# Dense products issued as one 128x128 matmul after a step of scores, in a two-round attention and feed-forward kernel

## The chip, the cores and the metric

The kernel runs on one core of one Trainium2 chip. The metric is the device time of one execution in microseconds. Before the change three runs gave 556.73, 559.66 and 559.98 us; the median, 559.66 us, is the time before.

## The reference, cut to what matters

There are 2048 tokens of width 512. One round is attention and then a gated feed-forward layer, each with a layer norm ahead of it and added to its input; two rounds run with the same weights.

```
x = x + _A_ref(_layernorm(x), A_wq, A_wk, A_wv, A_wo, A_beta)
x = x + _B_ref(_layernorm(x), B_w_gate, B_w_up, B_w_down)
x = x + _A_ref(...)      # the same again
x = x + _B_ref(...)
```

Attention has 32 heads of 16 channels. The tokens are cut into 4 segments of 512. Inside a segment it is causal softmax attention; beside it each head carries a memory over the segments: `M` (16x16) and `z` (16), from which `num = phi(q) @ M`, `den = phi(q) . z`, `a_mem = num / den`, and the result is `g * a_mem + (1 - g) * a_dot` with `g = sigmoid(beta)`. After each segment `M` and `z` grow by `phi(k)^T v` and the sum of `phi(k)`. The feed-forward layer is `gelu(x @ w_gate) * (x @ w_up) @ w_down` with 1792 hidden channels.

## The kernel before, in words

Two rounds of four segments make eight blocks `k = 0..7`. A block has projections to q, k and v, its steps of scores, the products of probabilities and values (called flushes in the code), from the second segment on the products with the memory, the output projection, and the feed-forward products gate, up and down.

All of it is put in order by a program that runs when the kernel is built. The class `Clocks` keeps an estimate of TensorE's clock, `ck.pe`, and of the other engines' clocks, and the loop at line 1620 chooses, at each value of `ck.pe`, the next piece of work for TensorE: a step of scores if its operands are there and four of the eight PSUM banks are free, else the next instruction of an open item, else a new item by its due time (`DUE`, `BIAS`), else a filler product of ones (`warm`) that keeps TensorE at work. A table `CHANGES` alters the due times and slacks at every 8 us of that clock. When the clock says that a result is there decides also which of VectorE and ScalarE empties a bank, and in which order these two, GpSimd and the DMA queue on SyncE get their work. The engines then run on the chip in the order that was built, each at its own pace, tied by semaphores.

TensorE's instructions use the 128x128 array in three shapes, which the text below calls by short names:

- **rows**: a step of scores (`visit`, line 1406, matmuls at line 1421). Four matmuls at once, each with 16 or 32 of the array's rows and all 128 columns (`tile_position=(32 * j, 0)`), one for each of four heads.
- **columns**: four matmuls at once, each with all 128 rows and 32 columns (`tile_position=(0, 32 * c)`). The flushes have this shape since each head has 32 output columns (line 1117, in `flush_item`), and in the kernel before so has every dense product: `product` (line 649, matmul at line 654) cuts one 128x128 product into four column strips. `dense` (line 656), `grown` (gate and up, line 1246), `piece` (down) and the filler call it, and so do the memory's products (`den_mm`, `mm` and `m` in `mem_items` and `upd_item`) and the transposes of `turn_item`.
- **whole**: one matmul with all rows and columns. In the kernel before only the 14 first fillers (line 552) and 16 transposes at the start (line 752) have it.

`Clocks.tiling(mode)` (line 338) adds `SWITCH = 0.108` us to `ck.pe` when the shape differs from the last one that was told to it; `visit` tells it "rows", `product` and `flush_item` tell it "columns".

Of the kernel before, what the change touches and what calls it, by code (L numbers as in the profile page):

```python
# [18 lines left out]
P = 128  # L19
# [7 lines left out]
KT = D // P  # L27
FF = 1792
FT = FF // P
# [430 lines left out]
def kernel(  # L460
# [14 lines left out]
    nc = tc.nc  # L475
# [52 lines left out]
    warm = cst.tile([P, P], BF16, name="warm")  # L528
    wide = warm[:].unsqueeze(1).to_broadcast([P, 4, P])
# [58 lines left out]
    def values_of(va, b, par, j):  # L588
        c = (16 * par + 4 * b + j) * (DH + 1)
        return slice(c, c + 32)  # L590
# [55 lines left out]
        ck.act.post(ck.made(), slack + tn.ACT_EVICT, (0.602, lambda: nc.scalar.activation(  # L646
            out=dst(), in_=src(), func=ACT.Copy), end), taken=taken)

    def product(out, lhsT, rhs, start=True, stop=True):

        ck.tiling("columns")
        for c in range(4):
            r = slice(32 * c, 32 * c + 32)
            nc.tensor.matmul(out[r], lhsT=lhsT[:, r], rhs=rhs, start=start, stop=stop, tile_position=(0, 32 * c))  # L654

    def dense(ps, pairs):
        n = len(pairs)
        return [(Clocks.MM[512], lambda i=i, l=l, r=r: product(ps()[:], l(), r(), i == 0, i == n - 1))
                for i, (l, r) in enumerate(pairs)]


# [106 lines left out]
    class Att:  # L768
# [319 lines left out]
        def flush_item(self, b, par, half):  # L1088
            k = self.k
            ps = Psum()  # L1090
            whole = half is None
# [18 lines left out]

            def mm():
                ck.tiling("columns")
                for n, (p, u, ki, q0, q1, step, c0) in enumerate(pieces):
                    shift = 0 if whole else HALF * p - HALF * half
                    va = vS if u == 2 else self.vaug
                    for j in range(4):
                        nc.tensor.matmul(ps()[32 * j:32 * j + 32, q0 + shift:q1 + shift],  # L1117
                                         lhsT=va[:, ki, values_of(va, b, p, j)],
                                         rhs=step["pt"][:, j, c0:c0 + q1 - q0], start=n == 0,
                                         stop=n == len(pieces) - 1, tile_position=(0, 32 * j))  # L1120
# [73 lines left out]
            rows = range(TPS) if whole or half else range(2)  # L1194
# [9 lines left out]
    class Ffn:  # L1204


        def __init__(self, k):
# [8 lines left out]
            def add_to_x(j, ps, slack, told, c=slice(0, D)):  # L1216
                xt, width = x_sb[:, self.tt0 + j, c], c.stop - c.start
                ck.dve.post(ck.made(), slack, (0.683 - 0.00104 * (D - width), lambda: nc.vector.tensor_tensor(  # L1218
                    out=xt, in0=xt, in1=ps()[:, 0:width], op=ALU.add), lambda t: (ps.read(t), told(t))))

            def loaded(name):
                return k > 0 or ("loaded", name) in ev
# [17 lines left out]
            def cols(h):  # L1240
                return slice(L * h // self.parts, L * (h + 1) // self.parts)

            def tiles(g):
                return range(self.parts * g, self.parts * g + self.parts)

            def grown(w, ps, g, h):
                return [(Clocks.MM[512] / self.parts + 0.0012 * (self.parts - 1),
                         lambda kt=kt, f=f, n=n: product(ps()[:, n * L // self.parts:(n + 1) * L // self.parts],
                                                         w[:, kt, f * P:(f + 1) * P], self.norm.xnT[:, kt, cols(h)],
                                                         kt == 0, kt == KT - 1))  # L1250
                        for n, f in enumerate(tiles(g)) for kt in range(KT)]

            def hidden(g, h):
# [62 lines left out]
            def down(j, c=slice(0, D)):  # L1316
                ps = Psum()
                h, width = j * self.parts // TPS, c.stop - c.start

                def piece(ft):  # L1320
                    product(ps()[:, 0:width], self.gel[:, ft, j * P:(j + 1) * P], wd_sb[:, ft, c], ft == 0, ft == FT - 1)
# [58 lines left out]
    def room_of(parts):  # L1380
        return both if sum(u == 2 for _, u, *_ in parts) > 1 else plain
# [24 lines left out]
    def visit(got):  # L1406
        k, t, parts, ends = streams.pop(0)
        a = att[k]
        step = room_of(parts).take()
        for i in got:  # L1410
            banks[i], owner[i] = 1e9, "s"
        for b, u, ki, q0, q1, c0 in parts:
            a.pts[b, u, ki, q0] = (q1, step, c0)
            step["left"] |= a.uses[b, u, ki, q0]
            for j in range(4):
                rows = slice(32 * j, 32 * j + (32 if u else 16))
                if u == 2:
# [3 lines left out]
                nc.tensor.matmul(big[:, got[j], c0:c0 + q1 - q0], lhsT=lhsT, rhs=a.q[rows, b, q0:q1], start=True,  # L1421
                                 stop=True, tile_position=(32 * j, 0))
        ck.tiling("rows")
        begun = ck.pe
        ck.on_pe(ck.STEP + ck.PART * (len(parts) - 2))
        width = max(c0 + q1 - q0 for _, _, _, q0, q1, c0 in parts)
        even = WHOLE and got[3] - got[0] == 3
        exp_and_mask(step, parts, got, [slice(0, 4)] if even else [slice(0, 2), slice(2, 4)], width, begun + 0.4)
        for f in ends:
            a.flush_item(*f)  # L1430
        if not any(st[0] == k for st in streams):
            ev["scores", k] = ck.pe
        if not any(st[0] == k and any(part[1] == 2 for part in st[2]) for st in streams):
            ev.setdefault(("shared", k), ck.pe)
# [185 lines left out]
    while streams or items or opened or ck.busy():  # L1620
        if tn.turn(ck.pe):
            items.sort(key=tn.due)
        ck.serve()
        next_e()
        if step_ready() and four_banks() and timely():
            score()
            continue
        if opened:
            cost, fn = opened.ops.pop(0)
            fn()  # L1630
            ck.on_pe(cost)
            if not opened.ops:
                it, opened = opened, None
                it.done()
            continue
        if may_open():
            late = ck.pe - tn.FLUSH_WAIT
            got = next((it for it in items if (it.kind != "flush" or not streams or it.posted < late
                                               or plain.full() or both.full()) and it.ready()), None)
            if got:  # L1640
                opened = open_item(got)
                continue
        if may_open():

            if streams:
                ps = Psum()
                ps.bank = free_banks()[-1]
                owner[ps.bank] = "m"
                product(ps()[:], warm[:], wide)
# [35 lines left out]
```

## Time and profile before

| what | number |
| --- | --- |
| runs, lowest / median / highest | 556.73 / 559.66 / 559.98 us |
| profiled execution: span from first to last instruction | 554.7 us |
| median less that span | 5.0 us |
| TensorE busy (PE) | 540.0 us, 97% of the span, 13722 matmuls |
| VectorE (DVE) / ScalarE (ACT) / GpSimd (POOL) busy | 432.6 / 419.6 / 237.9 us |
| 16 DMA engines, mean rate | 55 GB/s |
| granted TensorE clock | 1.000 |

How to read it: the page gives the profiled execution its span, and the three runs are whole device times, so a time is the span and some 2 to 5 us around it. PE is TensorE's matmuls and PEld its weight loads. In a row of the trace, "L654" is a line of the kernel, "128\*32" the array's rows and columns that a matmul uses, "128x512" its output, "x16" how many such matmuls were merged; the first two numbers are the start and the length in us. The end of a matmul is modelled, and it lies behind the start of the next one, so a length from a row overstates the time that the matmul keeps the array; the distance between two starts does not.

### The profile page before, as it was taken

The numbers are of one execution on the slowest core, as the hardware profiler recorded it, in microseconds if no ns is written. First come the engines' busy times: TensorE is split into PE (matmuls) and PEld (weight loads), VectorE is DVE, ScalarE is ACT, GpSimd is POOL, SyncE is SP. The second block draws the span as 40 slices with busy tenths as digits, with TensorE's granted clock in tenths as the row PEclk, the third lists the DMA queues.
The fourth block names the chain that finished last, engine by engine and source line by source line (L and its number), as shares of the span: only waits on it lengthen the run. The fifth ranks groups of instructions, "written<-read, shape, count | busy, mean of one in ns | idle before, by whom it ended". The sixth has DMA issues, their size and how long they took to land.

```text
span 554.7 us, 29909 instructions
## 1 busy us (share of the span) xinstructions
PE 540.0 (97%) x13722; PEld 293.8 (53%) x13722; DVE 432.6 (78%) x830; ACT 419.6 (76%) x386; POOL 237.9 (43%) x416
## 2 busy tenths in 40 slices
PE   8999899989899999999999999999999999999997
PEld 4446754765345444454444444445455455545994
DVE  7998689869897978688896876589988697588162
ACT  3899789988799887977989787968869855960610
POOL 6469045257348334834475345164582334112000
PEclk9999999999999999999999999999999999999999
DMA  8767527013601132300315020333242004010001
GB/s 258 182 144 183 101 56 95 14 22 59 83 4 21 23 60 42 59 8 19 55 28 70 14 41 4 50 51 24 40 98 61 2 5 98 6 20 21 24 5 41
DMA packets 69775, 30.39 MB, mean 55 GB/s; under 512 B 55120, under 2 KB 69200, under 8 KB 69648
## 3 DMA queue, kind: packets, MB, share of 16 engines
q1 hardware_dynamic: 69504, 28.46, 26.8%
q8 instruction: 107, 1.75, 1.3%
q14 instruction: 20, 0.16, 0.1%
q10 hardware_dynamic: 144, 0.01, 0.0%
HBM read 9.71 MB, written 2.10 MB: 21 GB/s over the span
## 4 chain that ended last, share of the span: by engine, by line
PE 80%; DVE 9%; DMA 4%; ACT 3%; issue 2%; POOL 1%; SPq 0%; ACTq 0%; DVEq 0%; POOLq 0%
PE big L654 68%; PE big L1421 7%; PE big L1117 5%; ACT pt L1491 3%; DMA amT<-am 1%; DVE xn L713 1%; DVE byq L1145 1%; DVE st L677 1%; DMA xnT<-xn 1%; DVE ab L1153 1%; POOL pt L1464 1%; DMA vS<-vaug 1%; DMA x_sb<-in_A_x_dram 1%; DVE x_sb L1218 1%; DVE aT L1160 1%
## 5 line engine op out<-in xcount | busy, mean ns | idle before, releaser
L1491 ACT ACTIVATE pt<-big 128x2048 bf16<-128x2048 f32 (+1 forms) x151 | 272.8, 1810 | 68.8 <-PE big L1421 63.7
L1464 POOL TENSOR_SCALAR_AFFINE_SELECT pt<-pt 64x256 bf16<-64x256 bf16 (+4 forms) x302 | 151.9, 530 | 232.7 <-ACT pt L1491 231.4
L654 PE MATMUL big<-xnT,wu_sb 128*32 128x512 bf16 (+1 forms) x2240 | 105.6, 337 | 0.9 <-issue 0.9
L654 PE MATMUL big<-wd_sb,gel 128*32 128x512 bf16 (+2 forms) x1848 | 105.2, 373 | 0.0
L654 PE MATMUL big<-xnT,wg_sb 128*32 128x512 bf16 (+1 forms) x2240 | 104.7, 337 | 0.0
L1308 DVE TENSOR_TENSOR gel<-gel,big 128x512 bf16<-128x512 bf16 x112 | 75.0, 682 | 32.0 <-PE big L654 26.9
L654 PEld LDWEIGHTS <-wg_sb 128*32 128x32 bf16 x2240 | 57.5, 97 | 35.6 <-issue 4.6
L654 PEld LDWEIGHTS <-wu_sb 128*32 128x32 bf16 x2240 | 58.2, 97 | 34.1 <-issue 4.9
L654 PEld LDWEIGHTS <-gel 128*32 128x32 bf16 x1848 | 46.6, 97 | 43.3 <-issue 3.6
L1218 DVE TENSOR_TENSOR x_sb<-x_sb,big 128x512 bf16<-128x512 bf16 (+1 forms) x65 | 43.1, 668 | 25.6 <-PE big L654 25.3
L1145 DVE STREAM_TRANSPOSE byq<-big 128x512 f32<-128x512 f32 x64 | 45.2, 706 | 20.5 <-PE big L1117 20.0
L1117 PE MATMUL big<-pt,vaug 128*32 128x64 bf16 (+5 forms) x1152 | 45.0, 263 | 2.1 <-issue 1.9
L677 DVE BATCH_NORM_STATS2 st<-x_sb 128x6 f32<-128x512 bf16 x60 | 40.5, 675 | 0.4
L1273 ACT ACTIVATE gel<-big 128x512 bf16<-128x512 f32 x64 | 35.2, 605 | 4.5 <-PE big L654 4.3
L654 PE MATMUL big<-xnT,wq_sb 128*32 128x512 bf16 (+1 forms) x528 | 35.0, 373 | 2.0 <-DMA xnT<-xn 1.7
L654 PE MATMUL big<-xnT,wk_sb 128*32 128x512 bf16 (+2 forms) x528 | 34.4, 373 | 0.0
L654 PE MATMUL big<-wo_sb,aT 128*32 128x512 bf16 x512 | 32.3, 380 | 0.1
L654 PE MATMUL big<-wv_sb,xnT 128*32 128x512 bf16 x512 | 31.9, 380 | 0.0
L816 POOL TENSOR_SCALAR kS<-kf,maskA 128x256 bf16<-128x256 bf16 x28 | 29.3, 1046 | 3.7 <-PE big L1421 2.6
L816 POOL TENSOR_SCALAR kS<-kf,maskB 128x256 bf16<-128x256 bf16 x28 | 29.1, 1041 | 0.3
L1117 PE MATMUL big<-pt,vS 128*32 128x64 bf16 x960 | 28.0, 193 | 1.2 <-DMA vS<-vaug 1.2
L713 DVE TENSOR_SCALAR xn<-x_sb,mv,rs 128x512 bf16<-128x512 bf16 x64 | 27.3, 471 | 1.1 <-POOL rs L1509 0.9
(98 smaller groups left out, 643.0 us busy)
## 6 DMA issues: line engine op xcount, KB each, us to landing
vS<-vaug SPq DMA_DIRECT2D x16, 136.0 KB, 2.7
out_dram<-x_sb SPq DMA_DIRECT2D x15, 128.0 KB, 2.7
wg_sb<-in_B_w_gate_dram SPq DMA_DIRECT2D x8, 224.0 KB, 5.6
wu_sb<-in_B_w_up_dram SPq DMA_DIRECT2D x8, 224.0 KB, 3.8
kB<-kf SPq DMA_DIRECT2D x28, 64.0 KB, 2.6
wd_sb<-in_B_w_down_dram SPq DMA_DIRECT2D x7, 256.0 KB, 4.7
x_sb<-in_A_x_dram SPq DMA_DIRECT2D x3, 512.0 KB, 6.4
xnT<-xn SPq DMA_TRANSPOSE x48, 3.1
```

What stands on the lines that cost most here:

```text
L654: nc.tensor.matmul(out[r], lhsT=lhsT[:, r], rhs=rhs, start=start, stop=stop, tile_position=(0, 32 * c))
L677: nc.vector.bn_stats(out=self.st6[:, 0, :], in_=x_sb[:, self.tt0 + j, :])
L713: eng.tensor_scalar(out=xn[:], in0=x_sb[:, self.tt0 + j, :], scalar1=self.mv[:, j, 0:1], scalar2=self.rs[:, j, :], op0=ALU.subtract, op1=A ...
L816: eng.tensor_scalar(out=kS[:, b, :, :, u], in0=self.kf[:, b, :].rearrange("p (t h c) -> p t h c", h=2, c=Q)[:, :, 0, :], scalar1=(maskA, m ...
L1117: nc.tensor.matmul(ps()[32 * j:32 * j + 32, q0 + shift:q1 + shift], lhsT=va[:, ki, values_of(va, b, p, j)], rhs=step["pt"][:, j, c0:c0 + q ...
L1145: nc.vector.transpose(out=self.byq[:, c], in_=ps()[:])
L1218: ck.dve.post(ck.made(), slack, (0.683 - 0.00104 * (D - width), lambda: nc.vector.tensor_tensor(out=xt, in0=xt, in1=ps()[:, 0:width], op=A ...
L1273: return lambda: nc.scalar.activation(out=out(), in_=in_(), func=ACT.Gelu_apprx_tanh)
L1308: ck.dve.post(ck.made(), NORMAL, (0.683, lambda: nc.vector.tensor_tensor(out=hidden(g, h), in0=hidden(g, h), in1=banked(ps), op=ALU.mult), ...
L1421: nc.tensor.matmul(big[:, got[j], c0:c0 + q1 - q0], lhsT=lhsT, rhs=a.q[rows, b, q0:q1], start=True, stop=True, tile_position=(32 * j, 0))
L1464: nc.gpsimd.affine_select(out=v, in_=v, pattern=[[0, m], [by, size]], compare_op=ALU.is_ge, fill=0.0, base=by - 1, channel_multiplier=-1)
L1491: 0.172 + 0.000832 * width * len(banks_of), lambda g=g, st=st: nc.scalar.activation(out=pt[:, g, 0:width], in_=st, func=ACT.Exp, scale=SCA ...
```

## The change

Dense products get a new argument, `dense=True`, and a variable `array` remembers which shape TensorE was last given. A dense product is issued as one whole matmul if the shape is not "columns", that is from a step of scores on, until a flush or one of the memory's products (or a transpose) sets it back to "columns". After that, dense products are cut into four strips as before, until the next step of scores. On the whole branch `product` returns ahead of `ck.tiling("columns")`, so there the planner's clock is not told of any shape.

```diff
-    def product(out, lhsT, rhs, start=True, stop=True):
+    def product(out, lhsT, rhs, start=True, stop=True, dense=False):
 
+        if dense and array[0] != "columns":
+            array[0] = "whole"
+            nc.tensor.matmul(out, lhsT=lhsT, rhs=rhs, start=start, stop=stop)
+            return
+        array[0] = "columns"
         ck.tiling("columns")
         for c in range(4):
             r = slice(32 * c, 32 * c + 32)
             nc.tensor.matmul(out[r], lhsT=lhsT[:, r], rhs=rhs, start=start, stop=stop, tile_position=(0, 32 * c))
 
+    array = ["columns"]
...
     def dense(ps, pairs):
...
-lambda i=i, l=l, r=r: product(ps()[:], l(), r(), i == 0, i == n - 1))
+lambda i=i, l=l, r=r: product(ps()[:], l(), r(), i == 0, i == n - 1, True))
...
# flush_item, mm():
                 ck.tiling("columns")
+                array[0] = "columns"
...
# visit(), behind the matmuls of the scores:
         ck.tiling("rows")
+        array[0] = "rows"
...
# grown (gate, up), piece (down) and the filler of the main loop: the same True (dense=True)
```

In the changed kernel the whole branch's matmul is line 653, the strips' line 659, the scores' line 1429 and the flushes' line 1125. TensorE has 10009 matmuls (13722 before): 1243 of them are whole dense products, 1094 with an output of 128x512 and 149 with one of 128x256. The following rows are TensorE's instructions in program order; `aT`, `wq_sb`, `wk_sb` are operands of dense products, `kB`, `kf` of scores, `pt` and `vaug` of flushes.

First, TensorE behind a step of scores in block 0, before: the last matmul of the scores and one dense product (of the output projection), in four strips.

```order
L1421 MATMUL big<-q,kB_130 128x192
L654 LDWEIGHTS aT
L654 MATMUL big<-wo_sb,aT 32x512
L654 LDWEIGHTS aT
L654 MATMUL big<-wo_sb,aT 32x512
L654 LDWEIGHTS aT
L654 MATMUL big<-wo_sb,aT 32x512
L654 LDWEIGHTS aT
L654 MATMUL big<-wo_sb,aT 32x512
```

TensorE behind the same step of scores in the changed kernel:

```order
L1429 MATMUL big<-q,kB_130 128x192
L653 LDWEIGHTS wq_sb
L653 MATMUL big<-xnT,wq_sb 128x512
L653 LDWEIGHTS wq_sb
L653 MATMUL big<-xnT,wq_sb 128x512
L653 LDWEIGHTS wq_sb
L653 MATMUL big<-xnT,wq_sb 128x512
L653 LDWEIGHTS wk_sb
```

Each dense product is now one load and one matmul, and it is another product that stands there: a projection of the next block in place of the output projection.

Second, TensorE where dense products end and a flush begins, before (block 0, the key projection and then the flush):

```order
L654 LDWEIGHTS wk_sb
L654 MATMUL big<-xnT,wk_sb 32x512
L1117 LDWEIGHTS vaug_132
L1117 MATMUL big<-pt,vaug_132 32x256
L1117 LDWEIGHTS vaug_132
```

Such a place in the changed kernel (the query projection, then the flush):

```order
L653 LDWEIGHTS wq_sb
L653 MATMUL big<-xnT,wq_sb 128x512
L1125 LDWEIGHTS vaug_132
L1125 MATMUL big<-pt,vaug_132 32x256
L1125 LDWEIGHTS vaug_132
```

Before, both sides were columns and nothing changed shape between them; now the shape changes from whole to columns ahead of the flush.

Third, TensorE early in block 0, where the order itself moved. Before, the step of scores over `kB` is followed by projections:

```order
L1421 LDWEIGHTS kB_130
L1421 MATMUL big<-q,kB_130 128x256
L654 LDWEIGHTS wq_sb
L654 MATMUL big<-xnT,wq_sb 32x512
L654 LDWEIGHTS wq_sb
```

In the changed kernel the next step of scores follows it at once:

```order
L1429 LDWEIGHTS kB_130
L1429 MATMUL big<-q,kB_130 128x256
L1429 LDWEIGHTS kf
L1429 MATMUL big<-q,kf 128x256
L1429 LDWEIGHTS kf
```

The projections of queries and keys moved behind the next scores and their flush. From there on the two orders differ all along the program, on every engine, though each has the same dense products, scores and flushes; the changed one has 4 filler products more (53 in place of 49).

Counted over the whole of each order, the shape changes from one TensorE matmul to the next as follows:

| from > to | before | changed |
| --- | --- | --- |
| columns > rows | 145 | 85 |
| rows > columns | 144 | 26 |
| rows > whole | 1 | 117 |
| whole > rows | 0 | 58 |
| whole > columns | 3 | 61 |
| columns > whole | 1 | 1 |
| all | 294 | 348 |

More of the change, by code (lines that the diff above doesn't have):

```diff
@@ L654, in product @@
             nc.tensor.matmul(out[r], lhsT=lhsT[:, r], rhs=rhs, start=start, stop=stop, tile_position=(0, 32 * c))
+    array = ["columns"]
     def dense(ps, pairs):
         n = len(pairs)
-        return [(Clocks.MM[512], lambda i=i, l=l, r=r: product(ps()[:], l(), r(), i == 0, i == n - 1))
+        return [(Clocks.MM[512], lambda i=i, l=l, r=r: product(ps()[:], l(), r(), i == 0, i == n - 1, True))
                 for i, (l, r) in enumerate(pairs)]
@@ L1249, in grown @@
                                                          w[:, kt, f * P:(f + 1) * P], self.norm.xnT[:, kt, cols(h)],
-                                                         kt == 0, kt == KT - 1))
+                                                         kt == 0, kt == KT - 1, True))
                         for n, f in enumerate(tiles(g)) for kt in range(KT)]
@@ L1320, in piece @@
                 def piece(ft):
-                    product(ps()[:, 0:width], self.gel[:, ft, j * P:(j + 1) * P], wd_sb[:, ft, c], ft == 0, ft == FT - 1)
+                    product(ps()[:, 0:width], self.gel[:, ft, j * P:(j + 1) * P], wd_sb[:, ft, c], ft == 0, ft == FT - 1, True)
                 def told(t):
@@ L1648 @@
                 owner[ps.bank] = "m"
-                product(ps()[:], warm[:], wide)
+                product(ps()[:], warm[:], wide, dense=True)
                 ck.unread(Clocks.MM[512])
```

## The prediction, made before the changed kernel ran

> **What bounds the kernel now.** I read the page's busy shares first, then its chain of work that ended last.
>
> ```profile
> PE 540.0 (97%) x13722; PEld 293.8 (53%) x13722; DVE 432.6 (78%) x830; ACT 419.6 (76%) x386; POOL 237.9 (43%) x416
> ...
> PE 80%; DVE 9%; DMA 4%; ACT 3%; issue 2%; POOL 1%; SPq 0%; ACTq 0%; DVEq 0%; POOLq 0%
> PE big L654 68%; PE big L1421 7%; PE big L1117 5%; ACT pt L1491 3%; DMA amT<-am 1%; DVE xn L713 1%; DVE byq L1145 1%; DVE st L677 1%; DMA xnT<-xn 1%; DVE ab L1153 1%; POOL pt L1464 1%; DMA vS<-vaug 1%; DMA x_sb<-in_A_x_dram 1%; DVE x_sb L1218 1%; DVE aT L1160 1%
> ```
>
> TensorE has work for 97% of the span, and 80% of the chain is TensorE, 68% the dense products that the change touches. A share is a mean over stages, so I asked next for the busy time by stretch (columns: stretch, its length, then PE, PEld, DVE, ACT, POOL).
>
> ```profile
> 40.00:110.00 70.00, 65.22 (x2036) 43.05 (x2036) 58.83 (x123) 62.04 (x62) 31.04 (x53) 1.00 0.49 91
> 110.00:180.00 70.00, 66.17 (x1836) 35.90 (x1832) 56.84 (x107) 61.75 (x61) 40.57 (x60) 1.00 0.26 37
> 180.00:250.00 70.00, 69.67 (x1648) 34.30 (x1644) 57.76 (x107) 58.29 (x46) 33.01 (x59) 1.00 0.21 39
> 460.00:530.00 70.00, 70.00 (x1824) 43.12 (x1816) 41.94 (x81) 39.16 (x43) 10.19 (x29) 1.00 0.15 32
> ```
>
> From 180 us on TensorE is nearly without a gap. Between 40 and 180 us it waits for 4.78 + 3.83 = 8.6 us, and there ScalarE, with 62 of 70 us, is next in line. The clock is 1.00 throughout. TensorE's waits are small and few:
>
> ```profile
> PE big L654 <- issue: 2.9, 4, 1.5
> PE big L1117 <- issue: 1.9, 1, 1.9
> PE big L654 <- DMA xnT<-xn: 1.7, 3, 0.8
> PE big L1117 <- DMA vS<-vaug: 1.2, 1, 1.2
> ```
>
> So the time is the sum of what TensorE does, and what the change does to that sum is what it does to the time, unless it makes new waits.
>
> **What a change of shape costs.** "Busy" hides one thing: a matmul's record reaches past the start of the next one. The timeline of starts shows it.
>
> ```profile
> 16.14 1.05 PE L654 MATMUL big<-xnT,wq_sb 128*32 128x512 bf16 x16
> 17.01 1.05 PE L654 MATMUL big<-xnT,wk_sb 128*32 128x512 bf16 x16
> ...
> 27.05 1.90 PE L654 MATMUL big<-warm 128*32 128x512 bf16 x32
> 28.88 0.29 PE L1421 MATMUL big<-q,kf 16*128 16x256 bf16 x4
> 29.00 0.28 PE L1421 MATMUL big<-q,kB 32*128 32x256 bf16 x4
> 29.21 1.05 PE L654 MATMUL big<-xnT,wq_sb 128*32 128x512 bf16 x16
> ```
>
> Four products (16 strips) take 17.01 - 16.14 = 0.87 us from start to start: 0.216 us for a product in columns, 0.108 for half the width. The 8 fillers from 27.05 on are through at 27.05 + 8 x 0.216 = 28.78, and the scores start at 28.88: columns > rows costs 0.10 us. The last scores, 256 wide, need 0.108 from 29.00 on, to 29.11, and the projection starts at 29.21: rows > columns costs 0.10 as well. The same in the middle of the program:
>
> ```profile
> 202.34 1.68 PE L654 MATMUL big<-wo_sb,aT 128*32 128x512 bf16 x28
> 203.95 0.40 PE L1421 MATMUL big<-q,kB 32*128 32x64 bf16 x8
> 204.28 1.26 PE L654 MATMUL big<-wo_sb,aT 128*32 128x512 bf16 x20
> ```
>
> Seven products end at 202.34 + 1.51 = 203.85, scores at 203.95 (0.10); the step is 64 + 448 = 512 columns wide in all, 0.216, and 0.33 us pass until the next product (0.11). I take 0.10 us for each change, from 0.09 to 0.11. With 294 changes (the table of front) the kernel before spends 29 us, 5% of its span, on changing shape.
>
> **The change part by part.**
>
> *The products themselves.* The trace has whole products only at the start. The last fillers of line 552, at the full clock, in the timeline:
>
> ```profile
> 5.29 1.03 PE L552 MATMUL big<-warm 128*128 128x512 bf16 x4
> ```
>
> Four fillers take 1.03 us, of which the last record is some 0.38 (in the row at 16.14, 1.05 less three starts of 0.216 leaves 0.40): three starts in 0.65, 0.216 us each. A whole product keeps the array as long as four strips, weight load included, so the 1243 products that become whole gain and lose nothing. For the 149 of half the width I take 0 too, since the 128-wide whole transposes of line 752 start every 0.06 us (next fence). TensorE gets 3713 matmuls fewer; that could shorten the waits marked "issue", 4.8 us at most, and I keep it among the waits.
>
> *Changes of shape that the trace shows.* Whole > columns goes from 3 to 61, columns > rows from 145 to 85, rows > columns from 144 to 26. The last two cost 0.10 us as above. For the first, and for the pair that matters most, there is this stretch of the timeline:
>
> ```profile
> 9.62 0.41 DVE L713 TENSOR_SCALAR xn<-x_sb,mv,rs 128x512 bf16<-128x512 bf16 x1
> ...
> 9.76 0.29 PE L1421 MATMUL big<-q,kB 32*128 32x256 bf16 x4
> ...
> 10.08 0.40 PE L752 MATMUL big<-ident,xn 128*128 128x128 bf16 x4
> ...
> 10.70 0.40 PE L752 MATMUL big<-ident,xn 128*128 128x128 bf16 x4 [0.21 <-DVE xn L713]
> ...
> 11.02 0.62 PE L654 MATMUL big<-warm 128*32 128x512 bf16 x8
> ```
>
> Their lengths, in the answer on line 752 (shortest, median, longest in ns):
>
> ```profile
> L752 PE MATMUL big<-ident,xn x16: 219/219/230, 6.5 to 10.9; 128*128 128x128 bf16 x16
> ```
>
> The four transposes at 10.70 last 0.40 us with a last record of 0.219, so they start every 0.06 us and are through at 10.94; the filler in columns starts at 11.02. Whole > columns costs 0.08 to 0.09 us; I take 0.10 for it too.
>
> *Changes that it does not show.* Rows > whole goes from 1 to 117 and whole > rows from 0 to 58: 175 changes on which the answer hangs. The one of before stands in the fence: the scores at 9.76 need 0.108 us, to 9.87, and the transposes start at 10.08, 0.21 later. But their operand `xn` comes from VectorE at 9.62 + 0.41 = 10.03, so the 0.21 may be all wait. The price lies between 0 (nothing in the row excludes it) and 0.21. Between these ends I take 0.10, because every change that can be seen, three pairs with three different partners, costs 0.08 to 0.11, with little regard to what the shapes on either side are.
>
> The page "TensorEngine Tiling (Array Packing)" of the Trainium skill says under Key Properties that a change of tiling mode, not of the tile alone, drains TensorE, and its list of configurations has 128x128, 32x128 and 128x32 as three modes. The trace agrees for the three pairs above; no run here shows it for rows and whole. By that rule the change adds a drain ahead of most flushes and removes none, which is the forecast below.
>
> *The sum of the shapes.* 348 changes in place of 294, each 0.10 us: **+5.4 us**. The mechanism is plain: a stretch scores, products, scores has two changes of shape in either kernel; a stretch scores, products, flush, scores had two and now has three, since the products are no longer in the shape that the flush needs.
>
> *Fillers.* Four more, 4 x 0.216: **+0.9 us**.
>
> *The order.* On the whole branch the planner's clock is told no shape, so it no longer charges its 0.108 us there, and the order differs from block 0 on (the third pair of rows in front shows projections that moved behind the next scores and their flush). The same work is in both lists; what can differ is how long TensorE waits. If TensorE really pays for the changes that the planner leaves out, it runs later than planned, and the other engines have that much more time to feed it; so I expect no crowd of new waits. The bounds: down, the "issue" waits shrink, -3; up, the 6% of waits between 40 and 180 us reach 100 us further, +6. I take **+1 us**, near the middle, since the rows after 180 us show hardly any. ScalarE, the next engine in line, has the same steps to turn into exponentials, and the queues of SyncE and GpSimd carry the same transfers and masks, in another order.
>
> Together +7.3 us on the span of 554.7, so 562.0, and 5.0 around it as at the median: **567.0 us**, 1.3% slower. Its own range, with 0.08 to 0.12 for the 175 unseen changes (3.5 us either way) and the waits' ends, is 561 to 575.
>
> **The rivals.**
>
> *Rows and whole need no drain between them* (the other side). Both use all 128 columns undivided, and only the rows taken differ; the row at 10.08 allows it. Then 175 of the 348 changes are free and 173 remain: 17.3 us in place of 29.4, -12.1; fillers +0.9. Here the planner is right about TensorE, which runs faster, so waits grow between 40 and 180 us, where ScalarE already has 89% of the time: +5. Sum -6.2: **553.5 us**, from 548.5 to 559. Against it: no seen change is free, though one side of the pair whole > columns also has all its rows in use. The point from which it decides: with p for an unseen change, 173 x 0.10 + 175 p - 29.4 + 0.9 is zero at p = 0.064 us without new waits, at 0.04 with 4 us of them. Below that the kernel is faster.
>
> *Only one of the two directions is free.* Free into whole: 231 changes, -6.3 + 0.9 + 3 of waits, 557.3. Free out of whole: 290, -0.4 + 0.9 + 2, 562.2. For it: a drain may depend on what runs out. Against it: columns > rows and rows > columns cost alike.
>
> *The order is what costs.* As the forecast, but the projections arrive late all along and TensorE waits after 180 us too as it does between 40 and 180, at 6% over 130 us more: +7.8, **574.8 us**. For it: the two orders agree for the first steps only. Against it: TensorE's long run without a gap from 180 us on, in which VectorE and ScalarE have 58 of 70 us (the row from 180 to 250).
>
> *The change doesn't do what it says:* it says that the order is untouched, and the lists of instructions say otherwise; that is in the sums above. That the products do become whole is seen in the rows.
>
> **How the numbers follow.** A measurement of this kernel tells about 1% from no change: faster is under 554.1, slower over 565.3. Forecast 0.54, of which 0.39 lies over 565.3 and 0.15 under. Rows and whole free 0.30: 0.17 faster, 0.13 within 1%. One direction free 0.10, all within 1%. The order 0.06, slower. That gives faster 0.17, same 0.38, slower 0.45. The range goes from 551 (most of the free case) to 575 (the end of the forecast's range, which cuts the order's case in half).
>
> **What would show it.** In the profile after: behind a step of scores that waits for nothing, the first whole product starts 0.10 us after the scores' columns are streamed; by the rival it starts at once, with its weight load ahead of it beside the scores. Ahead of a flush that follows whole products there is a new 0.10 us. Whole products start every 0.216 us; if they start further apart, the first step of the sum is wrong. TensorE's waits between 40 and 180 us should stay near 8.6 us; twice that, or waits behind 180 us, and the order decides. A span under 550 us would mean that the 175 changes are free or nearly so.

## The result, and the profile after

Four runs of the changed kernel gave 563.51, 564.62, 566.40 and 566.50 us, a median of 565.51; four of the kernel before (the three above and 558.46) gave a median of 559.06. The ratio to before is 1.0136, with a 95% interval from 1.0095 to 1.0178. The change makes the kernel slower by 6.5 us; the forecast was +7.3 us on the span and 567.0 us. The sum came out nearly right, but two of its terms did not, and they had opposite signs; that is what the rest is about.

The page of the changed kernel: busy shares, the granted clock in 40 slices of 14 us, the queue that brings instructions (packets, MB, share), and the chain.

```profile
span 564.8 us, 22454 instructions
PE 550.5 (97%) x10009; PEld 281.1 (50%) x10009; DVE 431.9 (76%) x827; ACT 420.8 (75%) x388; POOL 235.4 (42%) x420
PEclk9999998799899999999999999999999999999999
q8 instruction: 78, 1.28, 1.0%
PE 91%; DVE 3%; ACT 3%; DMA 1%; POOL 1%; issue 1%; ACTq 0%; DVEq 0%; POOLq 0%
PE big L653 46%; PE big L659 30%; PE big L1429 8%; PE big L1125 7%; ACT pt L1500 2%; DMA xnT<-xn 1%; DVE x_sb L1226 1%; DMA x_sb<-in_A_x_dram 1%; DVE st L684 0%; DVE xn L720 0%; DVE byq L1153 0%; DVE st L1514 0%; POOL rs L1518 0%; DVE xnT L645 0%; ACT L1281 0%
```

TensorE is still the bound: 91% of the chain, where it had 80%. It has a quarter fewer matmuls and is busy 10.5 us longer. New are the 8, 7 and 8 in the row of the clock. The same stretches as before (length, then PE, PEld, DVE, ACT, POOL, granted clock, DMA share, GB/s):

```profile
40.00:110.00 70.00, 66.49 (x1194) 38.22 (x1196) 55.35 (x114) 59.55 (x60) 29.16 (x50) 0.93 0.47 90
110.00:180.00 70.00, 67.24 (x1453) 35.20 (x1449) 57.71 (x108) 61.16 (x57) 40.44 (x61) 0.98 0.19 35
180.00:250.00 70.00, 70.00 (x1182) 32.05 (x1175) 54.86 (x103) 60.75 (x55) 32.52 (x56) 1.00 0.22 38
460.00:530.00 70.00, 69.60 (x1323) 37.17 (x1325) 47.80 (x98) 36.85 (x34) 12.45 (x30) 1.00 0.15 32
```

Between 40 and 180 us TensorE waits 3.51 + 2.76 = 6.3 us (8.6 before), and behind 180 us hardly at all, as predicted. Its waits are other ones, though (us in total, times, longest):

```profile
PE big L1125 <- ACT pt L1500: 3.7, 2, 1.8
PE big L659 <- DMA xnT<-xn: 2.7, 1, 2.7
PE big L552 <- DVE warm L530: 1.1, 1, 1.1
...
PE big L659 <- issue: 0.3, 1, 0.3
```

The waits marked "issue", 4.8 us before, are down to 0.3; in their place stand two waits of 1.8 us for exponentials and one of 2.7 us for a transposed block. What comes with the latter shows in short stretches of the same kernel:

```profile
90.00:95.00 5.00, 2.31 (x112) 1.41 (x103) 4.28 (x9) 3.07 (x3) 2.32 (x6) 0.94 0.72 111
95.00:100.00 5.00, 4.18 (x61) 1.47 (x61) 1.70 (x3) 2.37 (x2) 0.78 (x2) 0.50 0.02 4
100.00:105.00 5.00, 5.00 (x75) 2.30 (x72) 3.39 (x8) 2.91 (x4) 0.78 (x2) 0.54 0.28 56
105.00:110.00 5.00, 5.00 (x90) 3.94 (x91) 4.37 (x7) 4.97 (x5) 0.78 (x2) 1.00 0.14 26
```

From 94.4 to 104.6 us TensorE is granted half its clock, and "busy" there is half the work. The 10.2 us of it cost up to 5.

**The price of the changes of shape after**, in the timeline of TensorE's starts:

```profile
69.08 1.03 PE L653 MATMUL big<-xnT,wq_sb 128*128 128x512 bf16 x4
70.04 0.29 PE L1125 MATMUL big<-pt,vaug 128*32 128x256 bf16 x4
...
199.74 1.67 PE L653 MATMUL big<-wd_sb,gel 128*128 128x512 bf16 x7
201.35 0.40 PE L1429 MATMUL big<-q,kf 16*128 16x320 bf16 x8
...
203.86 0.41 PE L1429 MATMUL big<-q,kS 32*128 32x64 bf16 x32
204.20 2.12 PE L653 MATMUL big<-wv_sb,xnT 128*128 128x512 bf16 x9
```

Whole > columns: four products end at 69.08 + 0.864 = 69.94, the flush starts 0.10 later. Whole > rows: seven products and the change take 201.35 - 199.74 = 1.61 us; before, seven in columns and the change took the same 1.61 (202.34 to 203.95). Rows > whole: a step over `kS` and the change take 0.34; before, the same step with columns behind it took

```profile
116.06 0.41 PE L1421 MATMUL big<-q,kS 32*128 32x64 bf16 x32
116.40 0.51 PE L654 MATMUL big<-xnT,wu_sb 128*32 128x256 bf16 x12
```

0.34 too. Over all starts of this kernel that waited for nothing, at the full clock and with 0.216 us taken for 512 columns, rows > whole costs 0.09 us (111 of them), whole > rows and columns > rows 0.096, whole > columns 0.093 and rows > columns 0.09. The pair that no row of before showed costs what all others cost.

### The profile page after: what moved, and what is told of

It reads as the page before. It is cut to its first block, busy times and chain, and to the rows that moved or that the text cites. A ratio compares the mean times of both kernels' runs of the same rounds, so it can differ in the third digit from the quotient of the medians.

```text
span 564.8 us, 22454 instructions
## 1 busy us (share of the span) xinstructions
PE 550.5 (97%) x10009; PEld 281.1 (50%) x10009; DVE 431.9 (76%) x827; ACT 420.8 (75%) x388; POOL 235.4 (42%) x420
## 4 chain that ended last, share of the span: by engine, by line
PE 91%; DVE 3%; ACT 3%; DMA 1%; POOL 1%; issue 1%; ACTq 0%; DVEq 0%; POOLq 0%
PE big L653 46%; PE big L659 30%; PE big L1429 8%; PE big L1125 7%; ACT pt L1500 2%; DMA xnT<-xn 1%; DVE x_sb L1226 1%; DMA x_sb<-in_A_x_dram 1%; DVE st L684 0%; DVE xn L720 0%; DVE byq L1153 0%; DVE st L1514 0%; POOL rs L1518 0%; DVE xnT L645 0%; ACT L1281 0%
## 5 line engine op out<-in xcount | busy, mean ns | idle before, releaser
L653 PE MATMUL big<-xnT,wg_sb 128*128 128x512 bf16 (+1 forms) x374 | 75.8, 354 | 0.1
L653 PE MATMUL big<-wd_sb,gel 128*128 128x512 bf16 x233 | 55.0, 380 | 0.0
L653 PE MATMUL big<-xnT,wu_sb 128*128 128x512 bf16 (+1 forms) x259 | 54.8, 356 | 0.0
L653 PEld LDWEIGHTS <-wg_sb 128*128 128x128 bf16 x374 | 34.7, 98 | 34.3 <-issue 4.3
L659 PE MATMUL big<-xnT,wu_sb 128*32 128x256 bf16 (+1 forms) x1204 | 51.5, 321 | 0.0
L659 PE MATMUL big<-wd_sb,gel 128*32 128x512 bf16 (+2 forms) x916 | 49.9, 366 | 0.0
L659 PEld LDWEIGHTS <-wu_sb 128*32 128x32 bf16 x1204 | 32.2, 97 | 11.3
L653 PEld LDWEIGHTS <-wu_sb 128*128 128x128 bf16 x259 | 23.2, 98 | 23.5 <-issue 4.2
L659 PEld LDWEIGHTS <-gel 128*32 128x32 bf16 x916 | 24.7, 97 | 18.0
L659 PE MATMUL big<-xnT,wg_sb 128*32 128x256 bf16 (+1 forms) x744 | 29.0, 307 | 0.3 <-ACT gel L1281 0.3
```

The source lines that it names most:

```text
L653: nc.tensor.matmul(out, lhsT=lhsT, rhs=rhs, start=start, stop=stop)
```

## The experiments

"Before" is the kernel before on the same chip in the same session: median 557.83 us beside the shape alone, the order alone, all whole and whole without an added change; 558.35 beside the padded, early, late and replanned kernels; 558.09 beside the one that was told the truth, the best version and the memory's products; 558.94 beside the one with cut products. Times are medians of 6 to 12 runs, ratios have 95% intervals.

**The shape alone.** The change, but the planner's clock is told "columns" as before, so that the order stays that of the kernel before.

```diff
+        ck.tiling("columns")
         if dense and array[0] != "columns":
             array[0] = "whole"
             nc.tensor.matmul(out, lhsT=lhsT, rhs=rhs, start=start, stop=stop)
```

> Whole products as in the change, but the planner's clock is told of columns as before, so that every engine has the order of the kernel before; only the shapes change: 349 changes of shape in place of 294. Theory (each change of shape costs 0.09 to 0.10 us whatever the pair, and the time is the sum): 55 x 0.095 = +5.2 us, ratio 1.009. Rival 1 (the new order is what costs, the shapes are free or hidden): 0 us, ratio 1.000. Rival 2 (rows and whole are cheaper than the other pairs): -5 us or less, ratio under 0.99.

Measured: 553.17 us, ratio 0.9908 (0.9873 to 0.9942). It is *faster*, against what I expected, with 55 changes of shape more than before.

```profile
PE 543.9 (99%) x10044; PEld 278.5 (51%) x10044; DVE 434.0 (79%) x830; ACT 418.7 (76%) x386; POOL 236.1 (43%) x416
...
q8 instruction: 78, 1.28, 1.0%
```

```profile
PE big L659 <- issue: 1.3, 2, 1.1
PE big L552 <- DVE warm L530: 1.1, 1, 1.1
PE big L1429 <- ACT pt L1500: 0.8, 3, 0.4
```

Since the order is the same, the two traces can be laid side by side at each step of scores. This kernel is ahead of the one before by 2.6 us at 61, 4.2 at 121 and 5.4 at 150 us, and then falls back, to 3.4 at 500 us. The fall is the price of the changes, less 0.8 us gained at 427 us: in the pieces between two steps of scores in which neither kernel waits, each added one costs 0.09 to 0.10 us, some 5.3 for all 55. The gain comes at single places before 150 us, where before had these waits and this kernel has none or less:

```profile
61.23 0.21 PE L1117 MATMUL big<-pt,vaug 128*32 128x64 bf16 x4 [1.88 <-issue]
...
71.87 0.29 PE L654 MATMUL big<-xnT,wu_sb 128*32 128x256 bf16 x4 [0.86 <-issue]
...
118.87 0.21 PE L654 MATMUL big<-zcols,phiq 128*32 128x8 bf16 x8 [1.51 <-issue]
```

So my theory that the products themselves gain nothing fell. A new one had to have three terms: changes of shape, the order, and something that fewer instructions gain.

**The order alone.** The changed kernel's order, with every dense product in four strips.

```diff
         if dense and array[0] != "columns":
             array[0] = "whole"
-            nc.tensor.matmul(out, lhsT=lhsT, rhs=rhs, start=start, stop=stop)
-            return
-        array[0] = "columns"
-        ck.tiling("columns")
+        else:
+            array[0] = "columns"
+            ck.tiling("columns")
         for c in range(4):
```

> The order of the changed kernel (the planner's clock is not told of the dense products behind scores), but every dense product in four column strips as before: 290 changes of shape in place of 294, 4 fillers more. Theory: 4 x 0.095 less and 0.9 more for the fillers, and what is left of the 6.5 us that the change cost after its shapes: +1 to +2 us, ratio 1.002 to 1.004. Rival 1 (the order is what costs): +5 to +6.5 us, ratio 1.009 to 1.012, with more waits of TensorE between 40 and 180 us.

Measured: 564.38 us, ratio 1.0111 (1.0078 to 1.0144). The order costs 6 us by itself. TensorE's waits and two stretches of it:

```profile
PE big L1124 <- ACT pt L1499: 3.7, 2, 1.8
PE big L658 <- DMA xnT<-xn: 2.6, 2, 1.3
PE big L658 <- issue: 2.2, 2, 1.7
PE big L658 <- ACT xnT L646: 1.6, 1, 1.6
...
PE big L658 <- DVE xnT L645: 0.8, 1, 0.8
...
PE big L1124 <- DVE xnT L645: 0.6, 1, 0.6
```

```profile
0.00:40.00 40.00, 36.13 (x678) 17.74 (x682) 34.13 (x81) 27.13 (x28) 21.87 (x43) 1.00 0.68 192
150.00:250.00 100.00, 97.11 (x2315) 47.58 (x2308) 76.74 (x144) 85.59 (x80) 49.42 (x80) 0.98 0.20 34
```

Before was busy 37.81 and 99.11 us in these stretches, at the full clock. Between the two profiled executions (561.8 - 554.7 = 7.1 us) the waits make 4.3 us ((561.8 - 542.8) - (554.7 - 540.0)), the half clock up to 1.7 (3.4 us of it from 152.5 us on), and four fillers 0.9. In the waits, two flushes that now follow their step of scores at once, at 31 and 140 us, wait 3.7 us for exponentials, and 3.0 us go to `xnT` from ScalarE and VectorE, while the "issue" waits are 2.6 us shorter. After 180 us the order loses hardly anything.

This kernel and the changed one have the same order, so they too can be laid side by side: the whole products put the changed kernel some 4.1 us ahead at 80 us. It is 1.3 behind at 110 (a wait longer by 1.4 and the 10.2 us of half clock), 0.4 ahead at 160 (by then each has lost another 3.4 us of half clock, and this order in strips waited longer at 150), and from there 3.4 us of changes bring it to 3.0 behind at the end.

**All dense products whole**, in the order of before: 140 changes of shape more, 47% fewer matmuls.

```diff
         ck.tiling("columns")
+        if dense:
+            nc.tensor.matmul(out, lhsT=lhsT, rhs=rhs, start=start, stop=stop)
+            return
         for c in range(4):
```

> The order of the kernel before, and every dense product whole, behind flushes too: 434 changes of shape, 140 more than before. Theory: 140 x 0.095 = +13.3 us, ratio 1.024. Rival 1 (the order is what costs): 0 us. A third reading, that a part of the added drains lies in waits that are there anyway: half of it, +6 us.

Measured: 560.87 us, ratio 1.0047 (1.0024 to 1.0070). There is no "issue" wait at all in its trace. At about 0.096 us each, 140 changes are 13.4 us, so the rest gains 7.4 us by the spans of the two profiled executions (560.7 - 554.7 = 6.0; this one was the slowest of its runs and has 3.4 us of half clock) and 10.4 by the medians (+3.0).

**Whole only where it adds no change**: 776 products in stretches that lie between two steps of scores with nothing else in columns.

```diff
+BETWEEN_SCORES = [(25, 45), (62, 72), (90, 111), ...]
...
         ck.tiling("columns")
+        number = next(count) if dense else -1
+        if any(a <= number < b for a, b in BETWEEN_SCORES):
+            nc.tensor.matmul(out, lhsT=lhsT, rhs=rhs, start=start, stop=stop)
+            return
```

> The order of the kernel before; whole only for the 776 dense products in the 62 stretches that lie between one step of scores and the next with nothing else between, so that the number of changes stays at 294, but 125 of them are now between rows and whole in place of rows and columns. Theory: 0 us, within 0.5, ratio 0.999 to 1.001. Rival 2 (rows and whole are cheaper): down to -12 us if free. A whole product that keeps TensorE longer than four strips would show as a gain or loss over 776 products: 0.01 us each would be 7.8 us.

Measured: 554.12 us, ratio 0.9936 (0.9908 to 0.9964). The changes stay 294, and the gain of 3.5 us in the trace all lies before 150 us. With 0, 55 and 140 more changes the three kernels fit one price of 0.09 to 0.10 us; none of them leaves room for a pair that is free.

**Whole products early or late only.** Two kernels ask where the gain is: the shape alone up to 150 us of the planner's clock, and the kernel of no added changes from 150 us on.

```diff
# early
-        if dense and array[0] != "columns":
+        if dense and array[0] != "columns" and ck.pe < 150.0:
# late
-        if any(a <= number < b for a, b in BETWEEN_SCORES):
+        if ck.pe >= 150.0 and any(a <= number < b for a, b in BETWEEN_SCORES):
```

> As e1_shape_alone up to 150 us of the planner's clock, strips after it, in the order of the kernel before: 19 changes of shape more than before (e1: 55 more). Theory: the gain lies in that stretch, so at its end the kernel is 5.4 us ahead as e1 is there, and no later change of shape eats it up: -5 to -6 us, ratio 0.989 to 0.991, at least as fast as e1. Rival (the gain is spread over all products): -2 us, ratio 0.996.

> As e4_between_scores, but only from 150 us of the planner's clock on, strips before it: 294 changes of shape as before. Theory: nothing to gain there, 0 to -1 us, ratio 0.998 to 1.000. Rival (the gain is spread over all products): three quarters of e4's, -2.5 us, ratio 0.995.

Measured: early 551.70 us, ratio 0.9886 (0.9853 to 0.9919); late 559.51, ratio 1.0029 (1.0001 to 1.0058). All the gain is early. Early alone pays for 19 added changes and not 55; it is 1.7 us shorter than the shape alone on the spans (549.7 against 551.4), but the intervals of the two ratios overlap. In the stretch from 40 to 150 us before was busy 101.95 us, and this kernel does more of the same list:

```profile
40.00:150.00 110.00, 107.22 (x2237) 62.42 (x2249) 97.05 (x195) 100.00 (x96) 56.91 (x93) 1.00 0.38 78
```

**The instructions put back, by loads**: the shape alone, with six weight loads of one column ahead of each whole product, so that TensorE gets as many instructions as before.

```diff
             array[0] = "whole"
+            for _ in range(6):
+                nc.tensor.ldweights(warm[:, 0:1])
```

> As e1_shape_alone, with six more weight loads of one column of ones ahead of each whole product, which the product's own load then replaces: the same shapes and the same order, but TensorE has as many instructions again as the kernel before. Theory (formed after e1 to e4: TensorE's instructions are fetched by DMA, in the stretch up to 150 us, where weights are loaded, they come too late, and whole products gain because there are fewer of them): the instruction queue carries 107 packets again in place of 78, the waits marked issue come back, and the gain of 8.6 us goes; what is left is the price of 55 changes of shape, +5 us on before, ratio 1.005 to 1.010. Rival (whole products gain in another way, for instance fewer semaphores or a shorter stay in the array): as e1, ratio 0.991.

Measured: 577.45 us, ratio 1.0360 (1.0317 to 1.0402). That is far more than the 5 us expected with the theory. The added loads cost TensorE time all over the program (weight loads are now 19% of the chain), so this does not single out the early waits: inconclusive.

```profile
PE 555.7 (96%) x9972; PEld 382.3 (66%) x17400; DVE 434.5 (75%) x830; ACT 420.9 (73%) x386; POOL 237.1 (41%) x416
```

**The instructions put back, by cutting**: the early kernel with each whole product cut into matmuls of 128 columns.

```diff
-            nc.tensor.matmul(out, lhsT=lhsT, rhs=rhs, start=start, stop=stop)
+            n = out.shape[1] // P
+            for c in range(n):
+                r = slice(P * c, P * c + P)
+                nc.tensor.matmul(out[:, r], lhsT=lhsT, rhs=rhs[:, c] if len(rhs.shape) == 3 else rhs[:, r],
+                                 start=start and c == 0, stop=stop and c == n - 1)
```

> As e7_early (whole products up to 150 us, 313 changes of shape), but each whole product is cut along its 512 or 256 moving columns into four or two matmuls of 128, each with its own weight load, so that TensorE has 13404 matmuls again (before 13722, e7 12609). At the 0.056 us from start to start of the transposes, the cutting itself costs 212 x 0.008 + 159 x 0.004 = 2.3 us. Theory (the gain is the number of instructions): the instruction queue carries 105 packets, the waits marked issue come back with e7's gain of 6.6 us: 551.7 + 2.3 + 4 to 6 = 558 to 560 us, ratio 1.000 to 1.004. Rival (it is the shape itself): 551.7 + 2.3 = 554 us, ratio 0.993.

Measured: 558.13 us, ratio 0.9990 (0.9958 to 1.0023). The gain is gone, but not in the way the test was made for. Side by side with before this kernel is still 3.0 us ahead at 126 us and 2.4 at 145, with one early "issue" wait of 0.22. The 128-wide pieces start every 0.056 us where a quarter of a 512-wide product takes 0.054, some 2.4 us for 1166 pieces; the rest goes here:

```profile
148.08 0.40 PE L663 MATMUL big<-xnT,wq_sb 128*32 128x512 bf16 x4 [2.48 <-DVE mv L697]
```

a wait for VectorE's mean and variance, and again 3.4 us of half clock, from 149.2 us on. The products 256 wide also got two pieces in place of four strips, so the count was not fully back (2822 matmuls between 40 and 150 us; 3116 before, 2237 in the early kernel). The test leaves the count open. What an "issue" wait is stands in the trace of before.

**What an "issue" wait waits for.** Queue 8 brings instructions in packets of 16 KB. Before has 13722 loads and 13722 matmuls; at 64 bytes each, 256 in a packet, that makes 27444 x 64 B = 1.756 MB, and its page has

```profile
q8 instruction: 107, 1.75, 1.3%
```

The changed kernel, with 20018 of them, has 78 packets, so the queue carries TensorE's code. Packet by packet the trace gives when each landed (start plus time). Set against the ends of the waits in before:

```
wait ends   its length   last packet of queue 8 landed   difference
   61.23       1.88            59.81                        1.42
   64.69       0.22            63.35                        1.34
   68.41       0.28            66.88                        1.53
   71.87       0.86            70.53                        1.34
  118.87       1.51           117.57                        1.30
```

Packets land 3.5 to 6.5 us apart between 40 and 180 us, and yet each wait ends 1.30 to 1.53 us behind one. Over all traces but the padded kernel's, 34 of the 35 "issue" waits longer than 0.16 us end 1.24 to 1.56 us behind a packet, and the last 2.22 (waits of just 0.16 us stand where a matmul's record is missing; so do nearly all of the 0.24 us in the padded kernel, where 72 records are missing, while its wait of 0.97 us ends 1.33 us behind a packet).

A count of TensorE's instructions leaves no room for chance. The first instructions behind these five waits are numbers 2497, 2753, 3009, 3265 and 6081 of its list (counted from 0; 6081 is the load of the matmul that waited): three steps of 256 and one of 11 x 256. In all 35 waits the number is 193 above a multiple of 256, with the missing records counted in. So this wait is TensorE waiting for the packet with its next instructions. In the nine traces with all records, 90% of the packets start from 1.0 us before to 1.4 us after TensorE enters the 256 instructions ahead of theirs, and none of these 812 blocks starts less than 1.2 us after its packet landed. The code thus comes about one packet ahead, and a wait arises where 256 instructions run too fast for that. It falls where many narrow matmuls follow each other: 128x64 in flushes, 128x128 and 128x8 in the memory's products. A strip product beside them in the same packet fills it with four times the instructions in the same time.

**Only the memory's products whole**, the rest as before (the products of `mm` and `m` get `memory=True` as `den_mm` does here):

```diff
         ck.tiling("columns")
+        if memory:
+            nc.tensor.matmul(out, lhsT=lhsT, rhs=rhs, start=start, stop=stop)
+            return
...
-                product(den()[:, j, b, :], self.phiq[:, b, j * P:(j + 1) * P], mem_state[k - 1][1][:, b, :])
+                product(den()[:, j, b, :], self.phiq[:, b, j * P:(j + 1) * P], mem_state[k - 1][1][:, b, :], memory=True)
```

> The kernel before in its order and its strips, only the memory's products whole (den_mm, mm, m; 1152 strips become 288 matmuls), at whatever price in shapes: 345 changes, 51 more. Theory (instructions come too late at the memory's products in the first 150 us): 51 x 0.096 = +4.9, and the waits marked issue, 4.8 us, go or nearly so: 0 to +2 us, ratio 1.000 to 1.004. Rival (the waits have another cause than the number of instructions): +4.9 us, ratio 1.009, and the waits stay.

Measured: 559.32 us, ratio 1.0028 (0.9998 to 1.0058). Its fetch waits are half of before's (2.4 us), but 51 changes of shape are added, and two other waits are longer:

```profile
PE big L657 <- DMA xnT<-xn: 2.6, 2, 1.7
PE big L657 <- DVE mv L689: 2.5, 1, 2.5
PE big L1120 <- issue: 1.6, 1, 1.6
```

**Other orders.** Two kernels ask whether 6 us is much for an order. One is the kernel before with another price in the planner, the other is the change with the planner told the truth.

```diff
# replanned
-    SWITCH = 0.108
+    SWITCH = 0.100
# told the truth
             array[0] = "whole"
+            ck.tiling("whole")
```

> The kernel before, all products in strips, with one number of the planner's clock altered: the price of a change of shape 0.100 in place of 0.108 us. Theory: it is the leaving of this one order that costs, not what the planner is told, so another order costs about as much as e2's: +3 to +8 us, ratio 1.005 to 1.014. Rival (the order of the changed kernel is bad because the planner's clock leaves out what TensorE pays): a clock that is nearer to the 0.09 to 0.10 us of the trace costs nothing, ratio 0.997 to 1.002.

> The changed kernel with the planner's clock told of whole products too, so that it charges 0.108 us for every change of shape that TensorE makes; the order is a new one again, with 357 changes of shape. Theory (any other order than that of the kernel before costs): shapes 63 x 0.096 = +6, fewer instructions -5 to -8, the order +6 to +14 as in e2 and e9: +4 to +14 us, ratio 1.007 to 1.025. Rival (the changed kernel's order is bad because its planner does not know what TensorE pays): the order costs nothing, -2 to +1 us, ratio 0.996 to 1.002.

Measured: 572.05 us, ratio 1.0252 (1.0206 to 1.0298), and 578.49 us, ratio 1.0366 (1.0332 to 1.0401), both beyond what I expected. Most of it is fillers, which the planner puts in where it has nothing else: the replanned list has 106 fillers in place of 49 (57 x 0.216 = 12.3 us), the other 124 (16.2 us). A price in the planner that differs by 8 ns makes the kernel 2.5% slower, and telling it the truth 3.7%. None of the three other orders is as fast as that of before. Without its fillers the replanned order costs 1.4 us, so these two do not show what an order costs in waits; they show that an order can lose far more than the +1 us that I took, and in fillers too.

**The best version**: the early kernel with the memory's products and the transposes whole too, where they follow a step of scores before 150 us (`mm`, `m` and the transposes get `dense=True` as `den_mm` does here).

```diff
-                product(den()[:, j, b, :], self.phiq[:, b, j * P:(j + 1) * P], mem_state[k - 1][1][:, b, :])
+                product(den()[:, j, b, :], self.phiq[:, b, j * P:(j + 1) * P], mem_state[k - 1][1][:, b, :], dense=True)
```

> As e7_early, and up to 150 us the memory's products and the transposes of turn_item may be whole too where they follow a step of scores: 308 changes of shape in place of 313, and fewer instructions where the memory's small products use them up fastest. Theory: 5 x 0.096 = 0.5 us and up to 1.5 us of waits less than e7: 549.7 to 551.2 us where e7 has 551.7, ratio on before 0.985 to 0.988. Rival (the small whole products are slower than their strips, since each needs a load of 128 columns): as e7 or up to 2 us slower.

Measured: 550.82 us, ratio 0.9884 (0.9848 to 0.9920): faster than both kernels, by 7.3 us against before in the median; from the early kernel it can't be told apart.

## Why the prediction was right, and where it was wrong

*The price of rows > whole and whole > rows* (taken as 0.10, bounds 0 and 0.21, the step on which the answer hung): right: 0.09 to 0.10 us in the profile after, and the same per added change in the experiments. By the Trainium skill ("TensorEngine Tiling (Array Packing)", Key Properties) every change of mode drains TensorE; the runs now show a price for this pair too, 0.09 to 0.10 us. 54 more changes cost 5.2 us, forecast 5.4. The rivals of free changes fall.

*The products themselves* (0, with the "issue" waits left among the waits, "4.8 us at most"): a whole product does keep the array as long as four strips (1.61 us for seven in both). But the bound was the place to look. Fewer instructions take away most of the fetch waits, 3.5 us in the order of before (4.8 to 1.3) and more with the waits on transfers that move with them, and in that order they outweigh the changes: the shape alone is faster. I saw "issue" rows, gave them a floor of -3, and did not ask what they wait for; the landing times in the same trace would have told.

*The order* (+1 us, "no crowd of new waits"): wrong by 5 us. The reason I gave, that a TensorE behind its plan leaves the others more time, did not hold at 31 us and 140 us, where products that had covered a wait moved elsewhere. My rival of the order had the nearer size (+7.8 on top of the +1, where 6 to 7 were measured) but the wrong place: it put the waits behind 180 us, where there are none. I had the lists of both orders; what I did not do is to go along the flushes and see which lost the products ahead of them.

*The half clock* was in no term. 13.7 us of it in the profiled execution cost at most 6.8 us of TensorE's time, and there it eats most of what the whole products gain in the changed kernel's order. The runs' clocks, 0.988, 0.994, 0.988 and 0.997, go with their times, 566.50, 564.62, 566.40 and 563.51.

*Fillers*: right, four, 0.9 us.

*The time around the span*: I added 5.0 us to a span of 562.0; the span was 564.8 and the time around it 1.7. The profiled execution of before had been the fastest of its runs, so the 5.0 was mostly spread between runs, and the two errors cancelled.

Together, on the spans: order +7.1 (561.8 - 554.7) and shape +3.0 (564.8 - 561.8, of which about +5.6 for 58 changes), where I had 1.9 with the fillers and 5.4. The 3.0 holds for these two executions alone: the changed kernel's was its slowest, with four times the half clock, and the other was the fastest of its runs. By the medians the order by itself costs 6.5 us and the changed kernel 6.5, so whole products in that order gain about what their changes cost, while in the order of before they gain 4.7 net. The two effects do not add. That the total change came within 1 us of the forecast is in good part luck: the order was put 5 us too low, and what fewer instructions gain was put at nothing.

What stays open: neither padding could tell the count of instructions from their spacing. The start of each packet with the block before it speaks for spacing, the time that 256 instructions take, but no experiment changed that alone. It is also open why the block's transfer at 92 us comes later in the changed order, which was not followed up.

## What to carry to other kernels

A change of shape of the array costs TensorE the same 0.09 to 0.10 us whichever two of these three shapes they are, so count the changes, and use one whole matmul in place of four strips where it adds none, above all close to runs of narrow matmuls. When an edit touches what a planner's clock is told, time the new order by itself with the old instructions: here it was worth more than the edit in the old order, with the other sign. An "issue" wait is no noise; set its end against the packets of the instruction queue.

## What the runs showed of the hardware that I had not expected

TensorE's code comes by DMA while the kernel runs, 256 instructions a packet, in before each packet 0.88 to 1.72 us on its way, and TensorE goes on 1.24 to 1.56 us after it landed in 34 of 35 waits; waits of up to 1.9 us come from it.

Half clock comes in multiples of 3.41 us (10.24 and 3.41 in the changed kernel), here with waits that are shorter than that: it starts 2.05 us into the wait of 2.71 us at 92.3, and 0.65 us behind the end of the wait of 1.84 us at 139.7. The Trainium skill ("TensorE: Matmul & The Clock Gate", Part 1) has the clock fall after at least one idle window of about 3.4 us. The length of a window agrees; here it came with waits of 1.3 (in the order alone, at 152 us) to 2.7 us, and did not with one of 1.88 us in before, which ended at 61.23, so the length of a wait alone does not decide.
